# Fold buffers at fixed places inside the up-product buffers, and a new order of steps, in a fused Nyström attention and multiplicative FFN kernel

## The chip, the cores and the metric

The kernel runs on one core of one Trainium2 chip. The metric is device time in microseconds. Five engines take part, each with a queue of its own that it works off in order: TensorE (PE: matmuls, each with a weight load, PEld), VectorE (DVE), ScalarE (ACT), GpSimd (POOL) and SyncE (SP), which here issues transfers only. POOL and ACT issue some as well.

## The reference

```python
# attention: q, k, v are (8, 8, 576, 64); m = 32 landmarks, scale = 1/8
q_lm = q.reshape(B, H, m, S // m, D).mean(axis=3); k_lm = ...   # likewise
A, Bm, C = sm(q, k_lm), sm(q_lm, k_lm), sm(q_lm, k)             # softmax(scale * a @ b.T)
Z = Bm.T / (norm1(Bm) * norminf(Bm) + 1e-6)
for _ in range(6): Z = 2 * Z - Z @ Bm @ Z
x = (A @ Z @ C @ v)           # then heads side by side: (4608, 512)
# multiplicative feed-forward
out = ((x @ w1) * (x @ w2)) @ w3 @ w_out
# w1, w2: (512, 1024); w3: (1024, 1024); w_out: (1024, 512); all float32
```

## The kernel before

**The fold.** Since nothing stands between w3 and w_out, the kernel multiplies them first into w34 (1024 x 512) and needs one product afterwards. Each operand is split into two fp16 parts (high and low), so a block takes three matmuls. `split(c)` (S, L508) makes the two halves of w_out block c in the tile `wsp`. `turned_w3(j, cc)` (T, L515) transposes four 128x128 pieces of w3 block j on PE (L523), and ACT (L527) and DVE (L529) write the two halves to a `w3t` tile. `product(j)` (F, L533) runs 24 matmuls (L537) in eight steps and copies the result to w34 (L540). `load_w3` (L) and `load_wout` (LO) fetch the float32 blocks into `w3f` (three buffers) and `wof` (six buffers).

**The attention**, batch by batch (8 batches, all 8 heads at once): loads of q and k in halves (LQ, LK, on POOL's queue), of v (LV, on SP's), turns on DVE (TQ, TK, L165), landmark sums (SQ, SK: on DVE for batch 0, else on POOL, L194 to L205), `exchange` (E, L212/L223), scores of landmarks (B), norms (N), squares (R), six steps of the inverse (I0 to I5, for one to three batches together), scores C and A (L280, L333), values (V, L347), normalise (M, L366 to L375), landmark_values (Z, L415 to L423).

**The feed-forward.** `project` (G0 to G3, L438) forms Z C v w1 and Z C v w2 for a batch (32 landmarks of each head); ACT (L443) or DVE (L445) writes it to `gt`. `up(st, j)` (U0 to U7) multiplies ahat with one 128-column part of each projection (L453), ACT copies the first (a_sb, L458) and DVE multiplies it with the second, into `ab` (L460): a tile of 8 x 1152 for two batches, two buffers. `down(n)` (W, 36 of them, 128 rows each) multiplies ab with w34 (L495), ACT writes o_sb (L501), and SP sends it out in two pieces (L505). The last, n = 35, is cut into two halves (L476 to L490).

**Memory.** The fold's tiles (`wsp`, four `w3t`, three `w3f`, six `wof`) lie in a pool `pf`. The `ab` buffers lie in a pool `pab` that is opened when the first U is met, after `pf` has been closed: they take its place, and the first U can write only when the fold's tiles have been read for the last time. PSUM holds three tiles `big` of two banks, one bank `small` (scores_b, norms, squares, landmark_values and product 1) and one bank `acc` (the other products, and the downs).

**The order.** Nothing is scheduled automatically. Each of the functions above is a generator, and the string `ORDER` names, word by word, which one goes on by one step. The instructions enter each engine's queue in that order. K is one warm-up matmul, KC one step of `constants()` (L605), GT a tiny copy on POOL that waits for a weight block and so holds back the loads queued behind it, FV and P the same before v of batch 0 and w3 block 4, LW a half load of w1 or w2. The first loads (w3 blocks 0 and 1, w_out blocks 0 to 5) and the load of ACT's function table stand ahead of ORDER.

```python
    for word in ORDER.split():
        if word not in live:
...
            work = started(word)
...
            live[word] = work
        if live[word] is not None:
            next(live[word], None)
```

Of the kernel before, what the change touches and what calls it, by code (L numbers as in the profile page):

```python
# [7 lines left out]
FP32 = mybir.dt.float32  # L8
# [6 lines left out]
B = 8  # L15
H = 8
# [16 lines left out]
T0.0 S.0 S.0 T0.0 T0.0 T0.0 T0.1 S.2 S.2 LQ0.0 T0.1 K LQ1.0 S.1 T0.1 L.2 LO.6 S.3 F.0 K F.1 S.1  # L33
LK0.0 T0.0 KC F.0 LK1.0 T0.0 T1.0 F.0 T1.0 S.3 S.4 K T1.0 S.5 S.4 F.1 K FV.0 F.1 F.0 T1.1 T1.1 K S.6
F.0 S.5 T1.1 KC LO.7 KC F.1 F.1 T1.2 F.1 TQ1.0 T1.2 GT.0 LK1.1 L.3 T0.2 LK0.1 S.7 F.0 S.6 F.1 TQ0.0
T0.2 F.0 GT.2 S.7 T0.2 F.0 SQ0.0 T1.2 F.1 TK1.0 F.0 LQ1.1 LQ0.1 T1.3 P.4 T1.3 F.2 T1.3 F.2 SQ1.0
T0.3 GT.3 TK0.0 F.2 P.4 T0.3 LK1.2 SK0.0 L.5 F.2 T0.3 F.2 F.2 F.2 LK0.2 F.2 F.2 T0.4 F.1 T1.5 LQ1.2
KC SK1.0 F.3 F.3 T0.4 T1.5 F.3 TK0.1 FV.0 F.3 GT.4 T0.4 LW.1 TK1.1 L.6 E.0 F.3 F.3 E.0 B.0 T1.5 B.0
C.0 GT.5 F.3 B.0 F.3 C.0 N.0 T0.5 KC T1.4 TQ1.1 N.0 LW.0 F.3 T1.4 T1.4 SK0.1 C.0 TQ0.1 F.4 LV2.1 F.4
T0.5 F.4 A.0 T0.5 R.0 R.0 R.0 F.4 F.4 F.4 LQ0.2 A.0 I0.0 I0.0 T0.6 LV0.1 SK1.1 L.7 I0.0 A.0 T0.6 C.0  # L40
F.4 I1.0 M0.0 LQ1.3 I1.0 F.4 I1.0 I2.0 T0.6 KC SQ0.1 LW.0 F.4 T1.6 M0.0 F.5 F.5 I2.0 GT.6 I2.0 SQ1.1
M0.0 M1.0 C.0 TK1.2 F.5 V.0 V.0 TQ1.2 M1.0 T1.6 I3.0 F.5 F.5 TK0.2 I3.0 F.5 M1.0 I3.0 LK0.3 F.5 T0.7
F.5 T1.6 V.0 I4.0 V.0 F.5 T0.7 LV1.3 I4.0 F.6 F.6 E.1 F.6 TQ0.2 I4.0 I5.0 E.1 F.6 F.6 I5.0 T1.7 Z.0
SK0.2 Z.0 F.6 T0.7 A.1 Z.0 A.1 T1.7 F.6 F.6 TQ1.3 LQ0.3 A.1 SK1.2 LV3.1 LW.1 LK0.4 G2.0 G0.0 F.6 F.7
T1.7 F.7 G0.0 M0.0 C.1 TQ0.3 LK1.3 SQ0.2 M1.0 G2.0 F.7 C.1 F.7 F.7 C.1 F.7 F.7 C.1 C.1 LQ0.4 G3.0
SQ1.2 G1.0 E.2 E.2 LV1.1 F.7 U0.0 G3.0 B.1 U0.0 G1.0 V.1 U0.0 U4.0 B.1 V.1 TK0.3 U4.0 B.1 V.1 U0.0
U1.0 U4.0 N.1 TK1.3 V.1 LQ1.4 U5.0 U1.0 U4.0 N.1 U5.0 U5.0 U1.0 U2.0 U5.0 U2.0 SK0.3 U1.0 R.1 U3.0
R.1 R.1 U2.0 U3.0 LQ0.5 I0.1 U3.0 LK0.5 SK1.3 U2.0 I0.1 I0.1 U7.0 U3.0 I1.1 F.7 U7.0 I1.1 TK0.4 I1.1
U6.0 W.0 LV0.2 M1.1 U6.0 U6.0 M1.1 U6.0 U7.0 I2.1 U7.0 M0.1 M1.1 M0.1 W.0 I2.1 I2.1 A.2 LV2.2 LK1.5
LK1.4 W.0 I3.1 I3.1 W.1 A.2 I3.1 I4.1 M1.1 M0.1 I4.1 A.2 W.1 I4.1 W.1 I5.1 TQ0.4 I5.1 C.2 Z.1 C.2  # L50
Z.1 I5.1 M0.1 W.2 C.2 Z.1 G0.1 TQ1.4 TK1.4 G1.1 W.2 G0.1 W.0 G1.1 U0.1 U2.1 LV1.2 C.2 U0.1 U0.1 U1.1
W.2 U1.1 SQ0.3 SQ1.3 C.2 W.3 G2.1 SQ0.4 LV3.2 U0.1 U2.1 G3.1 G2.1 V.2 V.2 V.2 U2.1 G3.1 V.2 U1.1
U2.1 SQ1.4 U1.1 U3.1 LQ1.5 U3.1 W.3 TQ0.5 U3.1 SK0.4 U4.1 E.3 SK1.4 LV1.4 U3.1 Z.2 W.3 M0.2 U4.1 Z.2
U7.1 M0.2 U7.1 M0.2 LV2.4 LK1.6 U4.1 E.3 E.4 TK0.5 U5.1 U4.1 U7.1 LV3.3 W.2 LQ0.6 U6.1 U7.1 LV2.3
U5.1 LV3.4 U6.1 Z.2 W.4 E.4 TQ1.5 M1.2 M1.2 U5.1 U6.1 TK1.5 U5.1 B.3 G2.2 M1.2 U6.1 G1.2 G2.2 G0.2
G1.2 W.4 M0.2 G0.2 A.3 M1.2 W.4 G3.2 A.3 A.3 G3.2 LQ1.6 B.3 SK0.5 W.3 W.1 W.5 U3.2 U3.2 C.3 B.3
LQ1.7 C.3 W.5 N.3 LK0.6 W.4 SK1.5 U2.2 LV0.3 LQ0.7 U0.2 C.3 U0.2 N.3 LK1.7 C.3 R.3 U3.2 W.5 U3.2
U0.2 U2.2 U0.2 W.6 SQ0.5 U2.2 U4.2 U2.2 R.3 SQ1.5 U4.2 C.3 W.6 M0.3 M0.3 U1.2 U1.2 W.6 U4.2 U6.2
TQ0.6 V.3 U4.2 U6.2 R.3 V.3 U1.2 U1.2 U6.2 U6.2 W.7 LK0.7 U5.2 I0.3 W.7 U5.2 I0.3 U7.2 I0.3 TQ1.6
I1.3 TK0.6 I1.3 U7.2 W.7 V.3 U7.2 I1.3 W.5 I2.3 W.8 V.3 I2.3 I2.3 TK1.6 W.7 U7.2 I3.3 I3.3 I3.3 W.8  # L60
M1.3 I4.3 I4.3 W.8 LV0.4 U5.2 I4.3 W.9 U5.2 M1.3 I5.3 W.8 M1.3 A.4 M0.3 A.4 W.9 W.9 I5.3 I5.3 M1.3
Z.3 SK0.6 Z.3 A.4 W.6 W.9 C.4 W.10 M0.3 C.4 Z.3 G3.3 W.10 C.4 W.10 G1.3 G3.3 C.4 G0.3 G2.3 W.11 G0.3
U2.3 G1.3 G2.3 U1.3 U2.3 C.4 U2.3 V.4 U1.3 U2.3 SK1.6 E.5 U1.3 U0.3 TQ0.7 V.4 V.4 SQ0.6 LV2.5 U0.3
LV1.5 U1.3 E.5 TQ1.7 M0.4 V.4 U3.3 M0.4 U3.3 M0.4 U3.3 W.11 U0.3 TK0.7 U3.3 U5.3 TK1.7 W.11 U4.3
# [640 lines left out]
```

## Time and profile before

| what | value |
|---|---|
| runs shown, us | 260.65, 261.73, 262.62 (median 261.73) |
| profiled execution: span, us | 260.5; no separate time is given for it |
| granted TensorE clock, mean | 0.998 |
| instructions in the span | 10306 |
| PE / DVE / ACT / POOL busy, us | 249.7 / 161.5 / 159.2 / 119.3 |
| moved by DMA | 37.37 MB, mean 143 GB/s |
| costliest groups on PE, us busy | up L453 74.3; down L495 66.7; fold L537 41.6 |

The profile is one execution. Its page gives busy time by engine, the span in 40 slices, the chain of work that ended last, and groups of instructions by line (count, busy time, mean of one, and what ended the idle time in front of them). The trace behind it also answers by window, by line and by tile, and has the times at which transfers landed. Ends of matmuls are modelled, so a busy PE may still start matmuls slower than it could: the distance between the starts is the safer number.

### The profile page before, as it was taken

Reading aid. Unit: us, or ns where it says so; the run is one execution under the profiler, and the core shown is the slowest. Engines: PE = TensorE matmul, PEld = TensorE weight load, DVE = VectorE, ACT = ScalarE, POOL = GpSimd, SP = SyncE. Lnnn points to the kernel's source line nnn. Section 1 sums busy time; section 2 is a strip of 40 time slices with the busy share of each in tenths; the row PEclk is TensorE's granted clock in tenths of the full one; section 3 lists DMA queues with packets and bytes.
Section 4 is the critical chain, followed back from the end, with each engine's and each line's share of the span. In section 5 each row is a group of like instructions: output and inputs, shape, how many; then the busy total and the mean of one; then the engine's idle time right before and its main releaser. Section 6 shows DMA issues by size and latency. Waiting matters only on the chain.

```text
span 260.5 us, 10306 instructions
## 1 busy us (share of the span) xinstructions
PE 249.7 (96%) x4480; PEld 147.9 (57%) x4480; DVE 161.5 (62%) x306; ACT 159.2 (61%) x349; POOL 119.3 (46%) x199
## 2 busy tenths in 40 slices
PE   6999999989999999899999999999999999999993
PEld 2555554544476558546654764667666465756642
DVE  1579986526687787677658766466474643464510
ACT  3553363525656875995458899847764856456431
POOL 8060697989359989999079796000000000000000
PEclk9999999999999999999999999999999999999999
DMA  6999999999828827999346293130057231621355
GB/s 235 277 305 289 256 257 245 203 169 211 129 72 124 157 63 136 215 250 244 52 111 137 62 258 97 43 87 3 6 126 159 65 81 43 142 65 40 84 115 127
DMA packets 23357, 37.37 MB, mean 143 GB/s; under 512 B 2832, under 2 KB 11536, under 8 KB 23312
## 3 DMA queue, kind: packets, MB, share of 16 engines
q1 hardware_dynamic: 12928, 24.26, 35.6%
q0 software_dynamic: 9792, 11.54, 27.2%
q10 hardware_dynamic: 592, 0.92, 1.0%
q8 instruction: 35, 0.57, 0.9%
q14 instruction: 10, 0.08, 0.1%
HBM read 38.80 MB, written 9.44 MB: 185 GB/s over the span
## 4 chain that ended last, share of the span: by engine, by line
PE 82%; DVE 7%; ACT 5%; DMA 2%; issue 2%; SPq 0%; DVEq 0%; ACTq 0%
PE big L453 21%; PE acc L495 20%; PE acc L537 13%; PE big L438 5%; PE big L347 4%; PE big L389 4%; PE big L523 3%; PE small L537 2%; ACT a_sb L458 2%; DVE ab L460 2%; PE big L366 2%; PE big L495 1%; DMA wof<-in_moe_w_out_dram 1%; PE small L415 1%; PE big L326 1%
## 5 line engine op out<-in xcount | busy, mean ns | idle before, releaser
L453 PE MATMUL big<-ahat,gt 128*128 128x288 f16 x512 | 74.3, 286 | 1.3 <-ACT a_sb L458 0.7
L460 DVE TENSOR_TENSOR ab<-a_sb,big 128x576 f16<-128x576 f16 x64 | 47.1, 750 | 35.3 <-PE big L453 33.5
L495 PE MATMUL acc<-w,ab 128*128 128x512 f16 x264 | 66.7, 380 | 0.0
L453 PEld LDWEIGHTS <-gt 128*128 128x128 f16 x512 | 48.5, 98 | 22.0 <-issue 3.0
L458 ACT CAST a_sb<-big 128x576 f16<-128x576 f32 x64 | 40.2, 639 | 33.2 <-PE big L453 18.8
L194 POOL TENSOR_TENSOR tr<-qkT 128x256 f32<-128x256 f16 x56 | 37.3, 697 | 18.2 <-DVE qkT L165 16.3
L537 PE MATMUL acc<-wsp,w3t 128*128 128x512 f16 x168 | 41.6, 384 | 0.0
L495 PEld LDWEIGHTS <-ab 128*128 128x128 f16 x280 | 25.4, 98 | 27.0 <-issue 4.8
L537 PEld LDWEIGHTS <-w3t 128*128 128x128 f16 x192 | 18.4, 100 | 19.8 <-issue 3.1
L501 ACT ACTIVATE o_sb<-acc 128x512 f32<-128x512 f32 x33 | 19.8, 599 | 10.8 <-PE acc L495 9.5
L445 DVE TENSOR_SCALAR gt<-big 128x1024 f16<-128x1024 f32 x16 | 19.4, 1220 | 7.9 <-PE big L438 7.9
L165 DVE STREAM_TRANSPOSE qkT<-qkn 128x576 uint32<-128x576 uint32 x32 | 24.0, 762 | 0.0
L200 POOL TENSOR_TENSOR tr<-tr 128x256 f32<-128x256 f32 x28 | 19.8, 727 | 0.1
L443 ACT ACTIVATE gt<-big 128x1024 f16<-128x1024 f32 x16 | 15.7, 1024 | 3.4 <-PE big L438 3.3
L438 PE MATMUL big<-wup,zt 64*32 64x512 f16 x512 | 17.3, 379 | 0.3 <-ACT en L370 0.2
L347 PE MATMUL big<-vt,ent 64*32 64x64 f32 x1152 | 14.8, 225 | 0.1
L128 POOL DMA_DIRECT2D qkn<-in_k_dram x16 | 11.5, 722 | 6.9 <-DVE qkT L165 6.9
L347 PEld LDWEIGHTS big<-vt,ent 64*32 64x32 f32 x1152 | 12.7, 105 | 3.4 <-issue 2.3
L284 DVE STREAM_TRANSPOSE ent<-en 128x576 f32<-128x576 f32 x16 | 12.0, 762 | 3.3 <-ACT en L280 3.3
L375 DVE TENSOR_TENSOR ahat<-eat,en 128x576 f16<-128x576 f16 x16 | 13.8, 870 | 0.0
L280 ACT ACTIVATE en<-big 128x288 f32<-128x288 f32 x32 | 12.8, 415 | 0.5 <-PE big L269 0.5
L527 ACT ACTIVATE w3t<-big 128x512 f16<-128x512 f32 (+1 forms) x17 | 9.6, 571 | 5.6 <-PE big L523 5.3
(184 smaller groups left out, 302.8 us busy)
## 6 DMA issues: line engine op xcount, KB each, us to landing
out_dram<-o_sb SPq DMA_DIRECT2D x70, 128.0 KB, 2.4
qkn<-in_q_dram POOLq DMA_DIRECT2D x16, 288.0 KB, 8.5
qkn<-in_k_dram POOLq DMA_DIRECT2D x16, 288.0 KB, 8.9
vt<-in_v_dram SPq DMA_DIRECT2D x16, 288.0 KB, 4.8
vt<-in_v_dram SPq DMA_DIRECT2D x32, 144.0 KB, 4.6
w3f<-in_moe_w_dram SPq DMA_DIRECT2D x6, 512.0 KB, 9.1
wup<-in_moe_w_dram POOLq DMA_DIRECT2D x4, 512.0 KB, 14.7
wof<-in_moe_w_out_dram SPq DMA_DIRECT2D x6, 256.0 KB, 7.4
```

Of the source, the lines that this page charges most:

```text
L165: nc.vector.transpose(out=st["qkT"][:, t, prs].rearrange("p c r q e -> p (c r q e)").bitcast(U32), in_=st["qkn"][:, t, prs, :].rearrange(" ...
L194: add(out=tr[:, c], in0=x[:, c, 0:4, :], in1=x[:, c, 4:8, :], op=ALU.add)
L200: add(out=tr[:, c, 0:2, :], in0=tr[:, c, 0:2, :], in1=tr[:, c, 2:4, :], op=ALU.add)
L347: nc.tensor.matmul(psV[32 * o:32 * o + 32, qd, 0:64], ent[sl, pr, r, :], vt[sl, pr, 64 * r:64 * r + 64], start=(r == 0), stop=(r == RT - 1 ...
L438: nc.tensor.matmul(psG[o:o + 32, qd, :], zt[rs, i, h, :], wup[rs, h, w, fs], start=(i == 0), stop=(i == 1), tile_position=(64 * qd, o))
L445: nc.vector.tensor_scalar(out=g[:, :, w, fs], in0=psG, scalar1=1.0 / ZS, scalar2=None, op0=ALU.mult)
L453: nc.tensor.matmul(p[:, c, 0:HS], st["g"][:, qd, w, 128 * j:128 * j + 128], st["ahat", qd][:, c, :], start=(qd == 0), stop=(qd == 1))
L458: nc.scalar.copy(out=a_sb, in_=p[:, :, 0:HS])
L460: nc.vector.tensor_tensor(out=st["ab"][:, j, st["t0"]:st["t0"] + S].rearrange("p (c s) -> p c s", c=2), in0=a_sb, in1=p[:, :, 0:HS], op=AL ...
L495: nc.tensor.matmul(pso[:, :], ab[:, j, t0:t0 + 128], w34[:, j, :], start=(j == 0), stop=(j == 7))
L501: nc.scalar.activation(out=o_sb, in_=pso, func=AXF.Copy, scale=1.0 / (X64 * X64))
L537: nc.tensor.matmul(psW, w3ts[j, c // 4][:, a, c % 4, :], wsp[:, b, c, :], start=(c == 0 and a + b == 0), stop=(c == 7 and a == 1))
```

## The change

Four things change.

1. *Places.* The two up-product buffers, `abx` and `aby`, now exist from the start, and the fold's tiles are slices of them: `wsp` and one `w3t` lie in abx; the six `wof`, one `w3f` and one `w3t` (used once) lie in aby. Two `w3t` and two `w3f` have places of their own. Batches 0 and 1 write aby, 2 and 3 abx, 4 and 5 aby, 6 and 7 abx. From block 4 on, w3t rotates over three places; from block 3 on, w3f over two.
2. *PSUM.* `small` and `acc` become one name, `one`, with two buffers.
3. *Small instructions.* `squares` makes sz first and tz from it, for all batches in one instruction each (before: tz by one instruction per half and batch from PSUM). The tile `eye` goes; `bt` holds the unit matrix.
4. *Order.* ORDER is another one throughout. The leading loads and the table load become words of it (H, LO, AT). w_out block 3 is still issued from ACT's queue, now behind the table load, and shares a completion semaphore with the first half of w3 block 1, for whose landing its issue waits. Only the head of ORDER is shown.

```diff
 ORDER = """
-T0.0 S.0 S.0 T0.0 T0.0 T0.0 T0.1 S.2 S.2 LQ0.0 T0.1 K LQ1.0 S.1 T0.1 L.2 LO.6 S.3 F.0 K F.1 S.1
-LK0.0 T0.0 KC F.0 LK1.0 T0.0 T1.0 F.0 T1.0 S.3 S.4 K T1.0 S.5 S.4 F.1 K FV.0 F.1 F.0 T1.1 T1.1 K S.6
...
+H.0 LO.0 H.3 LK0.0 KC AT K LO.3 LO.1 K T0.0 T0.1 H.1 K P.4 LO.2 KC H.2 S.0 S.0 S.1 T0.0 T0.0 T0.1 K
+H.4 S.2 K T0.1 S.1 LO.5 F.0 T0.0 F.1 S.2 T0.0 S.3 F.1 T1.0 LO.4 T0.0 F.0 F.1 S.3 LK1.0 LQ1.0 S.4 L.2
...
-    def small():
-        return psp.tile([128, 512], FP32, name="small", bufs=1)
-
-    def acc():
-        return psp.tile([128, 512], FP32, name="acc", bufs=1)
+    def one():
+        return psp.tile([128, 512], FP32, name="one", bufs=2)
...
-        tz_ = ch["tz"] = pz.tile([128, 6, 32], FP32, name="tz_", bufs=2)
-        for i in range(2 * n):
-            nc.vector.scalar_tensor_tensor(out=tz_[:, i], in0=psR[:, 64 * i:64 * i + 32],
-                                           scalar=ch["nrn"][:, i:i + 1], in1=eye2, op0=ALU.mult, op1=ALU.add)
-        yield
         sz_ = ch["sz"] = pz.tile([128, 6, 64], FP32, name="sz_", bufs=2)
         nc.vector.tensor_tensor(out=sz_[:, x], in0=psR[:, 0:128 * n].rearrange("p (x m) -> p x m", m=64),
                                 in1=ch["nrn"][:, x].unsqueeze(2).to_broadcast([128, 2 * n, 64]), op=ALU.mult)
+        yield
+        tz_ = ch["tz"] = pz.tile([128, 6, 32], FP32, name="tz_", bufs=2)
+        nc.vector.tensor_tensor(out=tz_[:, x], in0=sz_[:, x, 0:32],
+                                in1=eye2.unsqueeze(1).to_broadcast([128, 2 * n, 32]), op=ALU.add)
...
-        w3t = w3ts[j, cc] = pf.tile([128, 2, 4, 128], FP16, name="w3t", bufs=4)
+        i = 2 * j + cc
+        w3t = w3ts[j, cc] = (w3t_at[i] if i < 4 else w3t_at[(i - 4) % 3]).rearrange(
+            "p (i c j) -> p i c j", i=2, c=4)
...
-    def open_ab(b):
-        if b // 2 not in pairs:
-            pairs[b // 2] = pab[0].tile([128, 8, 2 * S], FP16, name="ab")
-        sts[b]["ab"] = pairs[b // 2]
-        sts[b]["t0"] = S * (b % 2)
+    def open_ab(st):
+        b = st["b"]
+        st["ab"] = (aby, abx)[b // 2 % 2].rearrange("p (j t) -> p j t", j=8)
+        st["t0"] = S * (b % 2)
...
-    pf_scope = tc.tile_pool(name="pf", bufs=2)
-    pf = pf_scope.__enter__()
+    pf = ctx.enter_context(tc.tile_pool(name="pf", bufs=1))
+    abx = pf.tile([128, 16 * S], FP16, name="abx")
+    aby = pf.tile([128, 16 * S], FP16, name="aby")
...
-    wsp = pf.tile([128, 2, 8, DM], FP16, name="wsp", bufs=1)
+    wsp = abx[:, 0:16 * DM].rearrange("p (i c n) -> p i c n", i=2, c=8)
+    w3t_at = [pf.tile([128, 1024], FP16, name=f"w3t{i}") for i in range(2)] + [
+        abx[:, 16 * DM:16 * DM + 1024], aby[:, 16 * DM:16 * DM + 1024]]
+    w3f_at = [pf.tile([128, DF], FP32, name=f"w3f{i}") for i in range(2)] + [
+        aby[:, 12 * DM:16 * DM].bitcast(FP32)]
+
+    def place_w3(j):
+        w3f[j] = w3f_at[(0, 1, 2, 0, 1, 0, 1, 0)[j]]
...
-        wof[c] = pf.tile([128, DM], FP32, name="wof", bufs=6)
+        c6 = 2 * DM * (c % 6)
+        wof[c] = aby[:, c6:c6 + 2 * DM].bitcast(FP32)
...
+    def table():
+        nc.scalar.add_instruction(mybir.InstLoadActFuncSet(
+            name=nc.get_next_instruction_name(), act_func_set_id=6, engine=mybir.EngineType.Activation))
+        nc.scalar.activation(out=ready, in_=ident[:, 0:1], func=AXF.Copy, scale=WS)
+
+    def lead(n):
+        eng = nc.scalar if n == 3 else nc.sync
+        load_w3(n // 3, (slice(0, 256), slice(256, 512), slice(512, 1024), slice(0, 512), slice(512, 1024))[n], eng)
...
-            for qd in range(2):
-                nc.vector.tensor_copy(out=eye[sl, qd, :], in_=ident[sl, sl])
-            yield
-        nc.vector.tensor_tensor(out=eye2, in0=eye[:, 0], in1=eye[:, 0], op=ALU.add)
-        for i in range(6):
-            nc.vector.tensor_copy(out=bt[:, i, 32:64], in_=eye[:, 0])
+            nc.vector.tensor_copy(out=bt[sl, 0, 32:64], in_=ident[sl, sl])
+            yield
+        nc.vector.tensor_tensor(out=eye2, in0=bt[:, 0, 32:64], in1=bt[:, 0, 32:64], op=ALU.add)
+        for i in range(1, 6):
+            nc.vector.tensor_copy(out=bt[:, i, 32:64], in_=bt[:, 0, 32:64])
...
-            if word[0] == "U":
-                if not pab:
-                    pf_scope.__exit__(None, None, None)
-                    pab.append(ctx.enter_context(tc.tile_pool(name="pab", bufs=2)))
-                open_ab(int(word[3:]))
```

More of the change, by code (lines that the diff above doesn't have):

```diff
@@ L38 @@
[L38 to L52, printed above, removed]
@@ L85 @@
+W.33 W.32 W.27 W.32 W.34 W.27 W.33 W.34 W.35 W.32 W.34 W.31 W.33 W.32 W.31 W.35 W.31 W.34 W.35 W.35
+W.31 W.35 W.35
 """
@@ L230, in scores_b @@
     def scores_b(ch):
-        psB = small()
+        psB = one()
         n = ch["n"]
@@ L287, in norms @@
     def norms(ch):
-        psN = small()
+        psN = one()
         n, x = ch["n"], slice(0, 2 * ch["n"])
@@ L300, in squares @@
     def squares(ch):
-        psR = small()
+        psR = one()
         n, x = ch["n"], slice(0, 2 * ch["n"])
@@ L352, in values @@
         for qd, o, pr, sl in tiles:
-            nc.tensor.matmul(psV[32 * o:32 * o + 32, qd, 64:65], eye[sl, 0, :],
+            nc.tensor.matmul(psV[32 * o:32 * o + 32, qd, 64:65], bt[sl, 0, 32:64],
                              st["sums"][sl, pr:pr + 1], start=True, stop=True,
@@ L412, in landmark_values @@
     def landmark_values(st):
-        psZ = small()
+        psZ = one()
         for qd in range(2):
@@ L459, in up @@
                 yield
+        open_ab(st)
         nc.vector.tensor_tensor(
@@ L473, in down @@
                 c = slice(256 * half, 256 * half + 256)
-                pso = acc() if half else big()[:, 0, :]
+                pso = one() if half else big()[:, 0, :]
                 for j in range(8):
@@ L492, in down @@
             return
-        pso = big()[:, 0, :] if n > 30 and n % 2 else acc()
+        pso = big()[:, 0, :] if n > 30 and n % 2 else one()
         for j in range(8):
@@ L533, in product @@
     def product(j):
-        psW = small() if j == 1 else acc()
+        psW = one()
         for c in range(8):
@@ L598 @@
     mask4 = consts.tile([128, 4, 32], FP32, name="mask4")
-    eye = consts.tile([128, 2, 32], FP32, name="eye")
     ones4 = consts.tile([128, 128], FP16, name="ones4")
@@ L625, in paced_w3 @@
     def paced_w3(j):
-        w3f[j] = pf.tile([128, DF], FP32, name="w3f", bufs=3)
+        place_w3(j)
         nc.gpsimd.tensor_copy(out=w3f[j][:, 0:1], in_=sts[0]["qkn"][:, 1, 0, 0:1])
@@ L645, in started @@
             "S": lambda: split(n), "T": lambda: turned_w3(n, i), "F": lambda: product(n),
-            "P": lambda: paced_w3(n), "L": lambda: load_w3(n), "LO": lambda: load_wout(n, nc.sync),
+            "P": lambda: paced_w3(n), "L": lambda: load_w3(n), "LO": lambda: load_wout(n, nc.scalar if n in (0, 3) else nc.sync),
+            "H": lambda: lead(n), "AT": lambda: table(),
             "FV": lambda: first_v(), "LV": lambda: load_v(st, n, (i,)),
```

103 lines of the change are left out of this document (51 added, 52 removed).

## The prediction

> **What bounds the kernel now.** I read the page's busy shares first, then busy time by stretch, then the chain of work that ended last in order of time, then who waited for whom on PE, then single stretches of the timeline.
>
> ```profile
> PE 249.7 (96%) x4480; PEld 147.9 (57%) x4480; DVE 161.5 (62%) x306; ACT 159.2 (61%) x349; POOL 119.3 (46%) x199
> ...
> PE   6999999989999999899999999999999999999993
> ```
>
> TensorE has work nearly always, and the other engines a third of their time free. A shorter ACT or DVE instruction therefore pays only where PE stands still. Busy time by stretch shows where that is:
>
> ```profile
> 0.00:10.60 10.60, 8.26 (x23) 3.64 (x24) 3.73 (x13) 4.92 (x9) 5.31 (x19) 1.00 0.82 247
> 10.60:30.00 19.40, 19.40 (x107) 10.89 (x106) 16.43 (x37) 8.13 (x15) 6.67 (x14) 1.00 1.13 291
> 30.00:60.00 30.00, 27.88 (x472) 15.43 (x471) 18.74 (x47) 12.84 (x34) 26.71 (x45) 1.00 1.10 219
> ...
> 180.00:250.00 70.00, 69.90 (x1157) 42.46 (x1156) 37.51 (x57) 42.87 (x83) 0.00 (x0) 1.00 0.35 78
> 250.00:260.50 10.50, 6.42 (x38) 3.48 (x36) 0.42 (x1) 2.28 (x5) 0.00 (x0) 0.96 0.58 132
> ```
>
> The second number of a row is PE busy: 2.3 us are missing in the first stretch, 2.1 in the third, 4.1 at the end. The DMA share (last but one) is over 1 until 60 us: the transfers are the tight resource of the fold. The start, on PE:
>
> ```profile
> 4.16 0.66 PE L523 MATMUL big<-ident,w3f 128*128 128x128 f32 x2
> 5.97 1.54 PE L523 MATMUL big<-ident,w3f 128*128 128x128 f32 x6 [1.15 <-DVE w3t L529]
> ...
> 7.73 1.49 PE L537 MATMUL acc<-wsp,w3t 128*128 128x512 f16 x3
> ...
> 10.63 0.60 PE L537 MATMUL acc<-wsp,w3t 128*128 128x512 f16 x2
> ```
>
> Until 10.6 us a 128x512 matmul starts 0.43 us after the one before, from there 0.216. And the chain that ended last, at 35 to 40 us and at 52:
>
> ```profile
> 35.25 0.31 DVE eye L615
> 35.56 2.21 DVE bt L617 x6
> 37.78 0.68 DVE qkT L165
> ...
> 39.02 0.60 DVE w3t L529
> 39.66 0.52 PE big L326 x30
> ...
> 52.42 0.95 issue
> ```
>
> Six copies of constants stand in front of the w3t eviction on DVE, and the scores of batch 0 (A.0, L326) wait for it: PE stands for 1.24 us. At 52.0 it stands for 1.1 us with no releaser in the profile.
>
> I priced every pair of neighbouring matmuls at the median start-to-start time of that pair of lines (trace after 10.7 us). From the first matmul at 1.19 us this gives 241.7 us; the trace has 255.2. The 13.4 us between are PE's waits, by 20 us of PE work: 5.2, 1.4, 1.3, 0.8, 1.3, 0.7, 0.1, 1.3, 0.8, 0.4 and then none. That is all that a better order can win.
>
> **The change, part by part.**
>
> *PE work.* No matmul is added or dropped, 12 warm-ups stay. The new order priced alike is 0.2 us shorter: **-0.2**.
>
> *The head.* q and k pieces are issued after a pause: P.4's copy on POOL now stands behind the first k piece and waits for it (first landing before: 10.9). Weights come sooner: two pieces of 288 KB less lie ahead of the last w_out block, 2.1 us at the 276 KB/us of the first 11 us, so it lands near 16.5 and not 18.6. Against that, wof[3] is now issued from ACT's queue behind the table load and must wait for the first half of w3f[1], whose completion semaphore it shares (5.24 in the trace); S.0 stands behind it on ACT and starts near 5.7 instead of 4.23. First product: S.0 and S.1 (0.63 each), T0.0 (0.39), DVE's 0.42 after it, 7.8 us against 7.73. PE is then 3.7 to 4.7 us behind its priced work, before 5.2. But this is not kept. S.7's second half leaves DVE at 18.0 (16.5 + 0.63 + 0.69 and hops; before 20.6). Behind it DVE now has, with before's durations: eye2 0.31, five copies to bt 1.85, a turn 0.69, two memsets 0.46, L194 1.15, a w3t eviction 0.65, the k sums 1.94, two turns 1.43, an eviction 0.65, L194 1.15, the q sums 1.95: 12.2 us, so the landmarks of batch 0 are ready at 30.2 and exchange E.0 runs then. E.0 is at 25.4 of the priced work, so PE is 4.9 behind; before 31.7 against 26.5, 5.2. **-0.3** (from -1.5, if DVE is ready sooner, to +1).
>
> *Constants out of the path at 35 us.* Six copies become five and stand 15 us earlier (their price is in the 12.2). Between E.0 and A.0 only small waits are left: A.0's second bank waits for ACT's four exponentials, 1.5 us of L280 behind B.0's; I take 0.15 of 1.24: **-1.1** (0 to -1.24). Next late is the eviction of A.0 (0.65 twice), after which I.0 starts with some 0.3 to spare. The 16 small instructions of tz (0.24 each, L311) become 4, and tz now follows sz: DVE is the shorter by 3 us, and idle 38% of the time, so nothing is booked.
>
> *The wait at 52.0.* Unknown cause, so between 0 and -1.1; half: **-0.55**.
>
> *w3f and w3t buffers.* From w3 block 5 on only two places are left of three, and three of w3t. L.6 can be issued only when T1.4 is through, at 32.2 of the priced work, and T0.6 reads it at 38.9: 6.7 us for 512 KB. Before, it was issued at 24.5 and read at 45.5. SP's queue (L.6 and L.7), and the page's row of whole blocks with their median to landing:
>
> ```profile
> 24.49 0.35 SPq L566 DMA_DIRECT2D w3f<-in_moe_w_dram  x1
> ...
> 36.18 0.35 SPq L566 DMA_DIRECT2D w3f<-in_moe_w_dram  x1
> ```
>
> ```profile
> w3f<-in_moe_w_dram SPq DMA_DIRECT2D x6, 512.0 KB, 9.1
> ```
>
> These took 6.2 to 13.8 us by the landings. The 13.8 had 1.15 MB of v ahead in the same queue; once the transfer ahead had landed the last two took 2.6 and 4.0. In the new order L.5 and v's first pieces (22.5 on; 4.2 + 7.2 us by before's landings, and 1.8 for two pieces of batch 2) are through at about 37, when L.6 is issued: 5 to 6 us with the hop, no stall. With before's 9.5 the stall is 2.8. I take **+0.6**, ends 0 and 7.1.
>
> *v of batch 1.* Batch 2's first pieces take the spare v tile, so batch 1's six can start only after V.0: 50.7 to V.1 at 61.8 of the priced work, 11 us. Issue 3.9 us, the last landing 4.5 to 8.9 later (rows at 55.4 and 57.1): 0 to 1.7 late, **+0.4**.
>
> *Up under the fold and shared PSUM banks.* U0 starts at 60.3 of the work instead of 62.8, with 15 products still to run, so PE has filler; a product's or a down's bank may be reused out of turn. I listed for every wait of PE on ACT or DVE how far the PE work in between falls short of the instructions queued there (row durations plus 0.42 us for both hops). After 60 us of work the shortages sum to 7.4 before, where the trace has 5.4 of waits, and to 5.4 now: 4.0, so -1.4. At U0's start, however, ACT has gt (1.02), Ln (0.65), a_sb (0.64), four small exponentials (1.3) and gt again in one line, and U1 and U5 wait in turn; that adds 0.5. **-0.9** (-2.5 to +1.5).
>
> *The tail.* Down 31 now ends between the halves of down 35, and its two issues (0.59 each) stand on SP before the last one: **+0.5** (0 to 0.6). The 4.1 us after PE's last matmul stay.
>
> Sum: -0.2 - 0.3 - 1.1 - 0.55 + 0.6 + 0.4 - 0.9 + 0.5 = -1.55. The profiled execution has a span of 260.5 and no separate time; the runs shown have a median of 261.73, 1.2 above it, within their spread of 2. Against the median this is **260.2 us**.
>
> **Rivals.**
>
> *The w3 load is late.* L.6 takes the 13.8 us that it took before: stall 7.1, where 0.6 was booked, so 266.7. For: all six whole blocks took longer than the 6 us that I need. Against: the backlog ahead of it is gone by my count. It decides against the change from 8.8 us on (stall 2.1), and is over 1% slower from 11.4. The Trainium skill's page DMA: Bandwidth & Descriptors (Queues, rings and completion order) says that each DMA engine takes one queue's descriptors in ring order and goes round between the queues; by that rule L.6 can't pass v's pieces and shares with POOL's queue, which gives this rival's time if the backlog lasts. The landings agree: L.6 came 2.6 us after the last v piece.
>
> *More is won.* E.0 isn't held by DVE (-1.2 more), the 52.0 wait goes wholly (-0.55), no load is late (-1.0): 257.4. For: DVE has 12 fewer instructions. Against: E.0 stood right behind DVE's last sum before too (31.32 and 31.67).
>
> *The waits come back elsewhere.* The order is new in every place; if its later waits sum to before's 5.4 and A.0 waits as before, the -0.9 and -1.1 go: 262.2. For: the large waits at 107.3 (0.82) and 161.2 (0.57) stand at places that no short distance explains.
>
> **How the numbers follow.** Forecast 0.38 (its own range 258.8 to 261.5), more won 0.27, waits back 0.20, late load 0.15. About 1% is what a measurement of this kernel can tell from no change: 259.1 and 264.3. Faster: 0.27 and a quarter of the forecast, 0.36. Slower: most of the late load and a quarter of the waits, 0.20. Same: 0.44. Range 256.5 to 264.5: a little under the second rival, and into the lower end of the late load.
>
> **What would show it.** Right: E.0 (the two L212 matmuls) near 30, DVE's sums of batch 0 ending just before; no DVE copies before A.0; T0.6 (L523, near 44) without a wait; U0's first matmul near 66 to 67, before 70.7. Wrong: PE idle for microseconds before an L523 or before V.1's first L347; PE's last matmul after 257.

## The result, and the profile after

The changed kernel takes 260.07 us (median of 15 runs, 258.44 to 261.60), the kernel before 261.75 (15 runs, 260.65 to 262.62). The ratio is 0.9928, with a 95% interval of 0.9902 to 0.9954: 1.7 us, 0.7%, faster. The forecast was 260.2.

The profiled execution is the quickest of the 15: 258.44 us with a span of 256.7. In all of them the time is about 1.75 us above the span; so the trace of before, span 260.5, is of an execution of some 262.3 (an estimate), 0.5 above its median. The spans differ by 3.8 us, the medians by 1.7: the two traces overstate the gain, and part of the question is what the other 14 runs lose again.

Busy time by stretch of the changed kernel (the second number of a row is PE busy, the last but one the DMA share):

```profile
0.00:10.60 10.60, 7.95 (x35) 3.82 (x36) 4.37 (x15) 4.29 (x8) 3.20 (x16) 1.00 0.80 260
10.60:30.00 19.40, 18.33 (x96) 9.48 (x93) 16.70 (x40) 7.60 (x14) 8.54 (x16) 1.00 1.13 279
30.00:60.00 30.00, 29.14 (x510) 16.86 (x510) 18.98 (x39) 14.36 (x38) 27.94 (x45) 1.00 1.03 197
...
180.00:250.00 70.00, 69.92 (x1037) 42.18 (x1036) 34.43 (x51) 39.86 (x75) 0.00 (x0) 1.00 0.33 76
250.00:256.70 6.70, 2.23 (x15) 1.17 (x13) 0.42 (x1) 0.70 (x2) 0.00 (x0) 0.98 0.55 122
```

From 30 to 60 us PE misses 0.9 us and not 2.1. From 10.6 to 30 it now misses 1.1, where it missed nothing: the fold starts sooner and then waits for DVE, 0.5 us at 13 and 0.8 at 15 us.

With every pair of matmuls priced as in the prediction, PE's waits sum to 9.2 us (before 13.3, the sum of the prediction's list). By 20 us of priced work: 4.7, 1.4, 0.3, 0.9, 0.35, -0.15, 0.2, 0.7, 0.6, 0.1 and then about none. The first 40 us of work have 0.5 us less of waits than before, the next 20 have 1.0 less, the rest 2.6 (2.8 against 5.4).

The places that the prediction named, on PE, in order: E.0 (L210), A.0 (L323), T0.6 (the L523 at 44.99), V.1 (L344 at 69.01):

```profile
30.17 0.39 PE L210 MATMUL big<-lm,pick 128*128 128x256 f16 x2
...
34.86 0.57 PE L323 MATMUL big<-qkT,lm 32*32 32x288 f16 x20
...
44.99 0.63 PE L523 MATMUL big<-ident,w3f 128*128 128x128 f32 x4 [0.86 <-ACT sz__694 L399]
```

```profile
67.32 1.02 PE L450 MATMUL big<-ahat,gt 128*128 128x288 f16 x7
68.27 0.32 PE L344 MATMUL big<-vt,ent 64*32 64x64 f32 x10
69.01 0.59 PE L344 MATMUL big<-vt,ent 64*32 64x64 f32 x36 [0.41 <-DMA vt<-in_v_dram]
```

E.0 is at 30.17. The scores of batch 0 follow without a wait. T0.6 stands for 0.93 us over its priced step, V.1 for 0.62. The first up ran at 66.70 (in the kernel before at 70.74). So the prediction's sign "T0.6 without a wait" failed; those for E.0, the constants and the first up held. The end, PE's last matmul to the last instruction, took 4.4 us (in the kernel before 4.1).

### The profile page after: what moved, and what is told of

Its sections match the earlier page's. It is cut to its first block, busy times and chain, and to the rows that moved or that the text cites. A ratio compares the mean times of both kernels' runs of the same rounds, so it can differ in the third digit from the quotient of the medians.

```text
span 256.7 us, 10307 instructions
## 1 busy us (share of the span) xinstructions
PE 247.1 (96%) x4480; PEld 147.7 (58%) x4480; DVE 158.9 (62%) x289; ACT 158.9 (62%) x349; POOL 116.1 (45%) x199
## 4 chain that ended last, share of the span: by engine, by line
PE 84%; DMA 9%; ACT 2%; DVE 2%; issue 1%; SPq 1%; ACTq 0%; DVEq 0%
PE big L450 25%; PE one L493 23%; PE one L537 11%; PE big L435 6%; PE big L344 5%; PE big L386 4%; DMA vt<-in_v_dram 3%; DMA aby<-in_moe_w_out_dram 2%; PE big L523 2%; DMA w3f<-in_moe_w_dram 2%; PE big L323 1%; PE big L363 1%; PE big L267 1%; PE one L412 1%; DMA out_dram<-o_sb 1%
## 5 line engine op out<-in xcount | busy, mean ns | idle before, releaser
L458 DVE TENSOR_TENSOR abx<-a_sb,big 128x576 f16<-128x576 f16 x32 | 23.6, 752 | 21.8 <-PE big L450 16.4
L493 PE MATMUL one<-w,aby 128*128 128x512 f16 x144 | 37.0, 380 | 0.0
L458 DVE TENSOR_TENSOR aby<-a_sb,big 128x576 f16<-128x576 f16 x32 | 23.7, 750 | 16.9 <-PE big L450 14.2
L537 PE MATMUL one<-abx,w3t 128*128 128x512 f16 x120 | 29.9, 380 | 0.5 <-ACT w3t L527 0.5
L493 PE MATMUL one<-w,abx 128*128 128x512 f16 x120 | 30.0, 379 | 0.0
L499 ACT ACTIVATE o_sb<-one 128x512 f32<-128x512 f32 x33 | 19.6, 602 | 7.0 <-PE one L493 5.6
L442 DVE TENSOR_SCALAR gt<-big 128x1024 f16<-128x1024 f32 x16 | 19.4, 1216 | 7.1 <-PE big L435 7.1
L493 PEld LDWEIGHTS <-aby 128*128 128x128 f16 x144 | 12.8, 98 | 13.0 <-issue 2.7
L493 PEld LDWEIGHTS <-abx 128*128 128x128 f16 x136 | 12.9, 98 | 12.7 <-issue 1.5
L537 PEld LDWEIGHTS <-w3t 128*128 128x128 f16 x120 | 11.1, 98 | 12.3 <-ACT w3t L527 1.0
L344 PE MATMUL big<-vt,ent 64*32 64x64 f32 x1152 | 16.2, 224 | 0.5 <-DMA vt<-in_v_dram 0.4
L344 PEld LDWEIGHTS big<-vt,ent 64*32 64x32 f32 x1152 | 13.8, 105 | 3.9 <-issue 2.3
L537 PE MATMUL one<-abx 128*128 128x512 f16 x60 | 15.5, 379 | 0.4 <-DVE abx L510 0.4
```

The lines of the kernel that those rows point to most:

```text
L344: nc.tensor.matmul(psV[32 * o:32 * o + 32, qd, 0:64], ent[sl, pr, r, :], vt[sl, pr, 64 * r:64 * r + 64], start=(r == 0), stop=(r == RT - 1 ...
L442: nc.vector.tensor_scalar(out=g[:, :, w, fs], in0=psG, scalar1=1.0 / ZS, scalar2=None, op0=ALU.mult)
L458: nc.vector.tensor_tensor(out=st["ab"][:, j, st["t0"]:st["t0"] + S].rearrange("p (c s) -> p c s", c=2), in0=a_sb, in1=p[:, :, 0:HS], op=AL ...
L493: nc.tensor.matmul(pso[:, :], ab[:, j, t0:t0 + 128], w34[:, j, :], start=(j == 0), stop=(j == 7))
L499: nc.scalar.activation(out=o_sb, in_=pso, func=AXF.Copy, scale=1.0 / (X64 * X64))
L537: nc.tensor.matmul(psW, w3ts[j, c // 4][:, a, c % 4, :], wsp[:, b, c, :], start=(c == 0 and a + b == 0), stop=(c == 7 and a == 1))
```

## The experiments

| kernel | us, median (runs) | ratio to before, 95% interval | span of its trace |
|---|---|---|---|
| changed kernel | 260.07 (15) | 0.9928 [0.9902, 0.9954] | 256.7 |
| after_again | 259.41 (6) | 0.9899 [0.9867, 0.9931] | 257.7 |
| before_again | 261.89 (1) | - | 260.1 |
| before_consts_early | 261.13 (12) | 0.9981 [0.9959, 1.0003] | 259.3 |
| block6_place2 | 258.95 (6) | 0.9906 [0.9881, 0.9931] | 257.8 |
| v1_first | 259.68 (12) | 0.9938 [0.9914, 0.9962] | 259.5 |
| both | 258.17 (6) | 0.9864 [0.9837, 0.9892] | 254.9 |
| up_after_fold | 260.13 (12) | 0.9943 [0.9923, 0.9963] | 259.0 |
| both_up_after_fold | 260.26 (6) | 0.9935 [0.9916, 0.9955] | 258.5 |
| both_tail | 258.19 (6) | 0.9878 [0.9846, 0.9910] | 256.2 |
| before_order_fixed | 268.02 (6) | 1.0242 [1.0214, 1.0270] | 267.5 |
| before_order_places | 264.21 (8) | 1.0101 [1.0066, 1.0135] | 261.9 |
| before_32_more | 264.62 (1) | - | 262.8 |

**The two kernels once more: which waits are the order's, which are chance?**

after_again: no edit.

> The changed kernel unaltered, for a second trace and more times: its 15 times so far spread from 258.4 to 261.6 us, three times as wide as their effect. Theory: the spread comes from two transfers that TensorE waits for, the w3 load of block 6 (landed 44.85 us, 0.93 us of wait at 44) and the v pieces of batch 1 (0.87 us of waits at 68 to 70). Then a slower run of this kernel shows its whole excess over 256.7 in these two places, and the waits after 75 us stay at about 2 us by the priced positions. Rival: the excess is spread over many places after 75 us, as waits for DVE and ACT or for nothing that the profile shows.

before_again: no edit.

> The kernel before unaltered, for a second trace. Theory: of its waits, those that its order causes come back at the same place with the same size (1.24 us at 38 to 39.7 before the scores of batch 0), while the wait without a releaser at 52.0 (1.1 us) and the ones at 107.3 (0.82), 115.2 (0.52) and 161.2 (0.56) are chance: they come elsewhere, or not at all. Rival: all come back within 0.1 us, and so are properties of the order.

Of before, my theory fell. Every wait came back within 0.05 us: 1.24 and 1.20 before A.0, 1.11 and 1.08 without a releaser at 52, 0.82 at 107, 0.52 at 115, 0.44 at 158, 0.56 at 161. Only the first 20 us differ (5.2 and 4.6). The one at 107.3, for which I had found no reason, has a plain one: ACT does four copies of landmarks (L223) ahead of the evictions of up, whose bank the next up needs. In before (start, duration, what, and in brackets the wait and its releaser):

```profile
105.89 1.66 ACT L223 COPY lm<-lm 32x256 f16<-32x256 f16 x4
...
107.57 1.18 ACT L458 CAST a_sb<-big 128x576 f16<-128x576 f32 x2
...
108.26 0.94 PE L453 MATMUL big<-ahat,gt 128*128 128x288 f16 x6 [0.66 <-ACT a_sb L458]
```

Of the changed kernel, half held. The second trace is 1.0 us longer: 0.4 in the first 20 us and 0.8 at 68 to 71 us, less some 0.2 in small steps behind it; the wait of T0.6 is the same (0.94). So the place was right for V.1. The cause was not: all pieces of v had landed by 67.8, and PE stood from 69.80 to 71.49 with no releaser:

```profile
69.70 0.31 PE L344 MATMUL big<-vt,ent 64*32 64x64 f32 x10
71.49 0.64 PE L344 MATMUL big<-vt,ent 64*32 64x64 f32 x38 [1.48 <-issue]
```

**The constants, in the order of before.**

```diff
-LQ1.2 KC SK1.0 F.3 ... T0.5 KC T1.4 TQ1.1
+LQ1.2 KC KC SK1.0 F.3 ... T0.5 T1.4 TQ1.1
```

> The kernel before, with the step of its constants that copies the unit matrix into six tiles moved from behind the reciprocals of batch 0 (35 us) to right behind the fourth step (28.8 us), nothing else. Theory of the prediction: the 1.24 us wait before the scores of batch 0 goes, less what the copies now hold up on DVE ahead of the exchange: DVE's sums end 2.5 us later, so the exchange at 31.7 comes up to 2.5 us later. As the prediction books it, the copies are free only where DVE has no chain behind it; here they land in the 12 us chain before the exchange, so no gain, 0 to 1.5 us slower than the kernel before. Rival: the copies are the whole cost of the wait and are hidden at the new place: 1.1 us faster.

The trace shows both effects: A.0's 1.24 us are gone, and E.0 waits 0.39. Waits from 20 to 60 us of work fall from 2.7 to 1.9; the times by 0.5 us, with an interval that just reaches 1. So neither side came out: no loss, and less than the rival's 1.1. The copies were mispriced. They take 0.10 us each here and 0.37 at the old place:

```profile
29.15 0.19 DVE L615 TENSOR_TENSOR eye<-eye 128x32 f32<-128x32 f32 x1
29.26 0.60 DVE L617 COPY bt<-eye 128x32 f32<-128x32 f32 x6
```

The prediction's row has 2.21 us for the same six. At the old place POOL ran three tensor_tensor beside them; here POOL issues DMAs and copies one column. That POOL is the cause is inferred from these two rows.

**The late loads of the changed kernel.** block6_place2:

```diff
-        w3f[j] = w3f_at[(0, 1, 2, 0, 1, 0, 1, 0)[j]]
+        w3f[j] = w3f_at[(0, 1, 2, 0, 1, 0, 2, 1)[j]]
```

> The changed kernel with w3 block 6 in the third place (free since block 2 was turned) and block 7 in the place of block 4; the order of all instructions is kept. So the load of block 6 no longer waits for the turning of block 4. Theory: the 0.93 us wait of TensorE at 44 us is that load's landing (44.85 us), so it goes, and the time falls by 0.9 us against the changed kernel of the same chip. Rival: the wait is for ACT's copy of sz (the releaser that the profile names), and stays.

v1_first (words of ORDER):

```diff
-TQ0.1 LW.0 T0.5 LV3.2 I0.0 ... L.7 T1.6 T1.6 LW.1
+TQ0.1 LW.0 T0.5 LV3.1 I0.0 ... L.7 LV1.1 LV0.1 LV2.1 T1.6 T1.6 LW.1
-Z.0 LV1.1 T1.7 LV3.1 T1.7 ... LQ1.3 F.7 LV0.1 TK1.3 ... G1.0 LV2.1 F.7
+Z.0 T1.7 T1.7 ... LQ1.3 F.7 TK1.3 ... G1.0 LV3.2 F.7
```

> The changed kernel with the spare v tile given to batch 1 instead of batch 2: the two early pieces are those of batch 1, its other four follow block 7's load at about 40 us, and the two pieces of batch 2 come after them. Theory: the waits before the second product with v of batch 1 (0.87 us in the first trace, 1.78 in the second) go, the spread of the times narrows to about 1.5 us, and the median falls by 0.9 to 1.7. Rival: the four pieces now run beside the q and k pieces and the weights of the up products at 40 to 50 us, when the transfers are tight, and delay these: the gain is lost to a wait at 45 to 65 us.

both: these two edits.

> The last two edits together. Theory: they act at different places, so their gains add: 1.8 to 2.6 us less than the changed kernel, 257.5 to 258.5. Rival: with block 6 and the v pieces all early, one of them is late again, and less than either alone is left.

The wait of T0.6 was the load's. In block6_place2 its load is issued at 31.32 and not at 37.34 (SP's queue), and T0.6 (the L523 below) follows the step before it at once, at 44.08, though ACT's copy is where it was:

```profile
43.80 0.34 PE L386 MATMUL big<-sz__644,tz__630 32*32 32x64 f32 x16
44.08 0.66 PE L523 MATMUL big<-ident,aby 128*128 128x128 f32 x4
```

The profile had put the wait down to ACT only because ACT's copy (ending at 44.96) came 0.1 us later than the landing (44.85). The trace of block6_place2 is still longer than the changed kernel's: 0.73 us are new before V.0, where DVE is late (last section), and 1.27 and 0.94 without a releaser at 58.3 and 115.8. In v1_first the wait of T0.6 stays (1.31 us). Its wait for v is gone, and two without a releaser appear at 51.4 (1.28) and 58.6 (1.46). So neither edit alone moves the median beyond its interval. Together they do: 258.17, and the interval (up to 0.9892) lies below that of the changed kernel's 15 runs (from 0.9902), though not below that of its second six. both_tail, the same but for its last words, comes to 258.19. These two are the quickest versions found. In the trace of the kernel both, taken from the quickest of its six executions, PE is busy throughout from 30 to 100 us:

```profile
30.00:60.00 30.00, 30.00 (x515) 17.15 (x513) 19.06 (x40) 15.20 (x39) 28.83 (x45) 1.00 1.11 234
60.00:100.00 40.00, 40.00 (x970) 24.19 (x969) 29.39 (x52) 29.67 (x71) 34.62 (x58) 1.00 0.74 136
```

That isn't so in every execution: the trace of both_tail, with the same words up to there, has two waits without a releaser, 0.67 us at 50.8 and 1.19 at 57.9.

**Up under the fold.** In both kernels the last words of product 7 were put ahead of the first up (in the second, LV3.2 stands for LV2.1):

```diff
-G1.0 LV2.1 F.7 U0.0 M1.1 ... U1.0 F.7 TQ1.3 ... I0.1 F.7 I0.1 ... I1.1 F.7 TK0.4 ... I2.1 F.7 I3.1 ... E.3 F.7 SK0.4
+G1.0 LV2.1 F.7 F.7 F.7 F.7 F.7 F.7 U0.0 M1.1 ... U1.0 TQ1.3 ... I0.1 I0.1 ... I1.1 TK0.4 ... I2.1 I3.1 ... E.3 SK0.4
```

up_after_fold:

> The changed kernel with the five last words of the product of block 7 put ahead of the first up, as before; nothing else is moved. Theory of the prediction: up under the fold is worth part of the 0.9 us booked for it and the shared banks, so 0.3 to 0.9 us slower than the changed kernel, with waits for DVE or ACT between 72 and 82 us. Rival: TensorE had other work in these places too, and the time is the same within 0.2 us: then the gain after 60 us is the order's, not that of up under the fold.

both_up_after_fold:

> The two edits together, and the last words of the product of block 7 ahead of the first up. With the two late transfers out of the way, this gives the price of up under the fold alone. Theory: in up_after_fold the waits of TensorE for DVE and ACT between 70 and 85 us came to 1.75 us, where the changed kernel has none, and hid the late v; so here they stand alone, and the time is 1.0 to 1.8 us more than with both edits. Rival: less than 0.3 us, since other stages take up the same slack later.

In the changed kernel the difference is small and not clear of noise: 0.9943 against 0.9928 and 0.9899. Its trace says why: some 1.7 us of waits for DVE, ACT and the bank between 70 and 85 us are new, but V.1 comes later and no longer waits for its v. With the loads out of the way the price stands alone: 0.9935 against 0.9864, 1.9 us, and PE misses 1.6 us of 60 to 100 us, where both misses none:

```profile
60.00:100.00 40.00, 38.40 (x802) 22.14 (x801) 26.54 (x46) 27.88 (x68) 31.48 (x52) 1.00 0.71 135
```

The difference of the medians is a little above the 1.0 to 1.8 expected.

**The order of before on fixed places.** ORDER is that of before, with the leading loads (H, LO, AT) as words ahead of it; in the second kernel also:

```diff
-        w3f[j] = w3f_at[(0, 1, 2, 0, 1, 0, 1, 0)[j]]
+        w3f[j] = w3f_at[(0, 1, 2, 0, 1, 2, 0, 1)[j]]
-        w3t = w3ts[j, cc] = (w3t_at[i] if i < 4 else w3t_at[(i - 4) % 3]).rearrange(
+        w3t = w3ts[j, cc] = (w3t_at[i % 4]).rearrange(
```

before_order_fixed:

> The changed kernel's functions, fixed fold buffers, shared banks and five constant copies with the order of before (the leading loads as words in front of it): it parts the buffers from the order. Theory: the buffers alone allow, but don't bring: up still begins behind the fold, the constants' step still stands in front of the scores of batch 0, and the waits at 52.0, 107.3, 115.2 and 161.2 stay. Block 6 has one place less to go to, so its load waits for the turning of block 4. 261 to 263 us, no better than before. Rival: the shared banks or the fixed places themselves give the gain, 259 to 260.

before_order_places:

> before_order_fixed was to part the buffers from the order, but there the load of block 6 came ahead of the turning of block 4 in the same place, so that one product was of the wrong block and the time is not that of this order. Here the fixed places are used with the rotation of before (three places for w3, four for its turned halves, up behind the fold). So this is the order of before on fixed places, shared banks, five copies and the joined small steps. Theory: the order carries the gain; the waits at 107 (0.82), 115 (0.52), 158 (0.44) and 161 us (0.56) come back, and the time is 261 to 262.5. Rival: the places, banks and joined steps bring it, and the time is 259 to 260.

Neither computes the reference's result. In the first, block 6 is loaded into the place of block 4 ahead of the turning of block 4, so a product is of the wrong block. In the second, the second half of block 5 is turned into the place of block 3's second half ahead of product 3, and a product stands for 2.0 us at 38 us. And in both the head is another one (one wait of 2.9 us at 4.5). So their totals say nothing on the order. What can be read is the part after 60 us of work, where none of this enters: in the second kernel the waits sum to 5.3 us, in the kernel before to 5.4, and 0.82, 0.52, 0.45 and 0.55 stand at the same four matmuls. Shared banks, fixed places and joined steps do not take them away; another order does. Whether the order alone, in buffers of before, would be as quick wasn't tried: it needs up under the fold, which those buffers forbid.

**The wait without a releaser.** In before:

```diff
     for _ in range(7):
         warm_up()
+    for _ in range(16): nc.tensor.matmul(psw[:, 0, 0:32], warm[:, 0:128], warm[:, 0:32], start=True, stop=True)
```

> The kernel before with 16 short matmuls of 32 columns (16 weight loads and 16 matmuls, 32 more instructions on TensorE) behind the seven leading warm-ups. In all traces so far, TensorE's waits that have no releaser end at an instruction whose number in TensorE's trace leaves 192 when divided by 256: 960 (twice in the kernel before, at 52 us, and in v1_first), 1216, 1728, 3776. Theory: these are late fetches of TensorE's own instructions, 256 to a block; the instruction stream is what counts, so the wait near 52 us comes again in front of instruction 960 of the trace, now a matmul of the product of block 6, 16 matmuls earlier, of 0.5 to 1.5 us, and not in front of the turning of block 7. Rival: the turning of block 7 itself waits for something (its transfer, a copy of ACT): the wait stays in front of it, at instruction 992. About 1 us more than before either way.

It came in front of instruction 960, now inside an inverse step (L389), with 2.26 us. A second came at 149.5 us, in front of 5312, which also leaves 192. The turning of block 7 no longer waits. Both waits and the time were larger than expected: 2.26 us against 0.5 to 1.5, and 264.62 in this one run, 2.7 above the median of before, against about 1.

```profile
49.03 0.33 PE L389 MATMUL big<-sz__721,tz__718 32*32 32x64 f32 x12
51.62 0.30 PE L389 MATMUL big<-sz__721,tz__718 32*32 32x64 f32 x4 [2.26 <-issue]
```

Busy time from the start to the wait counts the matmuls (x behind the first busy time): 473 in before, at another matmul of the program 473 here, and 473 and 601 in v1_first, whose order is another again. 601 is 473 + 128, with as many weight loads: 256 instructions.

```profile
0.00:52.10 52.10, 48.59 (x473) 25.96 (x473) 36.60 (x89) 23.96 (x53) 31.50 (x65) 1.00 1.07 258
```

```profile
0.00:49.20 49.20, 45.89 (x473) 25.34 (x474) 35.85 (x87) 23.65 (x52) 29.63 (x61) 1.00 1.08 260
```

```profile
0.00:51.50 51.50, 47.27 (x473) 24.97 (x474) 36.98 (x86) 23.69 (x54) 32.18 (x64) 1.00 1.07 255
0.00:58.70 58.70, 53.39 (x601) 28.46 (x601) 38.78 (x89) 25.36 (x57) 37.91 (x74) 1.00 1.10 245
```

**The tail.**

```diff
-W.33 W.34 W.35 W.32 W.34 W.31 W.33 W.32 W.31 W.35 W.31 W.34 W.35 W.35 W.31 W.35 W.35
+W.33 W.34 W.31 W.32 W.34 W.33 W.31 W.32 W.31 W.34 W.35 W.31 W.35 W.35 W.35 W.35 W.35
```

> The two edits together, and down 31 finished ahead of the first half of down 35 as in the kernel before, so that no store of it stands on SP ahead of the last ones. Theory: from TensorE's last matmul to the end it is 4.7 us in the changed kernel and 4.4 before; this goes back to 4.4, 0.3 to 0.4 us less than with both edits. Rival: the stores of down 31 are hidden by the last matmuls, and no time is won.

From PE's last matmul to the end it is 4.15 us, with both 4.43: the 0.3 us are there. The medians (258.19 against 258.17) don't show them.

## Why the prediction came out as it did

The time was right to 0.1 us, and the sum less so: four of its eight terms were too small in size (the wait at 52.0, the w3 load, v of batch 1 and, by far the most, up and the banks), and one step stands on two errors that happen to cancel.

*PE work, -0.2.* Held as far as it can be seen: from 180 us on, priced and traced steps agree within 0.5 us in every trace.

*The head, -0.3.* E.0 was forecast at 30.2, 4.9 us behind its priced place; it came at 30.17, 4.8 behind, with DVE's last sum just done, so -0.4. But the chain to it was wrong in two links. "S.7's second half leaves DVE at 18.0": it left at 19.4 (row 18.71, 0.68 us), since splits and w3 evictions go by turns on ACT until 16.4 and on DVE behind it; the last w_out block was there at 14.9 (forecast 16.5; the 276 KB/us used for it is the rate from 6.5 to 13 us, that of the first 10.6 us is 247). And "five copies to bt 1.85": they took 0.52. One is 1.4 late, the other 1.3 short.

```profile
18.71 0.68 DVE L510 SCALAR_TENSOR_TENSOR abx<-aby,abx 128x512 f16<-128x512 f32 x1
19.31 0.19 DVE L614 TENSOR_TENSOR eye<-bt 128x32 f32<-128x32 f32 x1
19.41 0.52 DVE L616 COPY bt<-bt 128x32 f32<-128x32 f32 x5
...
29.62 0.50 DVE L203 TENSOR_TENSOR lm<-tr 128x128 f16<-128x128 f32 x2
```

*Constants out of the path at 35 us, -1.1.* The 1.24 us are gone. before_consts_early shows the step alone in the other order: 0.8 us in its trace.

*The wait at 52.0, -0.55.* It went wholly: -1.1 in this trace. "Unknown cause, so between 0 and -1.1; half" is a choice, not a price. In the kernel before it isn't chance: it came in both its traces and in before_consts_early. It isn't the order's alone either: in before_order_places, the same words in other buffers, the step cost 0.26. The last section has the cause as far as it is known.

*w3f and w3t buffers, +0.6.* Measured +0.93, and 0.90 to 1.31 in the four traces where block 6 has this place. It was issued at 37.34 (forecast 37.1) and landed 7.5 us later (forecast 5 to 6). v's last piece landed at 37.95, so hardly any backlog of its own queue was ahead of it; what was left was to share the engines with POOL's loads, at a DMA share of 1.12 until it landed. The Trainium skill's page DMA: Bandwidth & Descriptors (Queues, rings and completion order), weighed there, has both: order within a queue, turns between queues. The landings agree with it: v's last piece, this load (44.85) and the next (46.58) landed in the order of issue, and from 37.95 to 44.85 us POOL's queue took 66% of the engines and SP's 44%.

*v of batch 1, +0.4.* Measured +0.62 in one trace, 0 in the other (landed at 67.8, read at 68.76).

*Up under the fold and shared PSUM banks, -0.9.* Here the size failed. Waits after 60 us of work fell from 5.4 to 2.8 with V.1's 0.62 still in it: -3.2. "After 60 us of work the shortages sum to ... 5.4 now: 4.0, so -1.4" scaled the waits with a sum of shortages, as if they were spread evenly. But 2.3 us of them are four waits of before at 107, 115, 158 and 161 us, each at one place (at 107 behind ACT's four copies, at 161 behind ACT's exponentials), and the trace of the changed kernel has no wait over 0.25 us after 75 us. And "that adds 0.5" for U0, U1 and U5 did not come: PE had other work. How the 3.2 us divide between the order and up under the fold isn't known: put behind the fold, up costs 1.9 us in the kernel both, whose order was not otherwise changed for it.

*The tail, +0.5.* Measured +0.3.

The sum by the trace is -0.2 - 0.4 - 1.2 - 1.1 + 0.9 + 0.6 - 3.2 + 0.3 = -4.3, where the span fell by 3.8; the other 0.5 lies in steps that aren't placed. The medians differ by 1.7. Of the 2.1 between, 0.5 is that the trace of before is above its median, and 1.6 the median run of the changed kernel loses again. The forecast booked 2.7 us too little and had no term for this loss; that it met the median to 0.1 us is luck. The second trace shows where 1.0 us of the loss goes: 0.4 before 20 us, and 0.8 more at V.1, where a wait of 1.69 without a releaser stands for the 0.62 and 0.25 of the first trace, less the 0.2 behind it. The longest execution of this kernel, 262.05 us, wasn't traced.

Of the rivals, *the w3 load is late* had the right place and the wrong length. *More is won* (257.4) is nearer than the forecast to the profiled execution (258.44), but of its three grounds only the wait at 52.0 held: E.0 is held by DVE, and both loads are late. *The waits come back elsewhere* fell for the trace shown, and is right in one sense: some waits are fixed by no order, and come in one run and not in another.

## What to carry to other kernels

Take a second trace of the kernel before, ahead of any forecast: a wait that returns within 0.05 us belongs to the kernel and is a term of the sum at its full size, one that doesn't return needs a range of its own. Price an instruction from a row with the same neighbour on POOL, not only with the same shape. And when two late transfers are found, mend both before judging either: alone, neither edit here moved the median beyond its interval, since other waits stood in its trace.

## What the runs showed of the hardware

**TensorE waits for its own instructions.** All waits over 0.8 us without a releaser after 20 us, in twelve traces (all but those of before_order_fixed and before_order_places), stand in front of an instruction of PE whose number leaves 192 when divided by 256 (weight loads, matmuls and semaphore waits counted: 960, 1216, 1728, 3776, 5312). Queue q8 of kind "instruction" moves one packet of 16 KB per 256 such instructions, 35 in the kernel. It mostly starts soon after PE enters the block before: 1.1 us after in the median, from 1.3 us ahead to 6.1 after. In before, the one for the block at 960 lies in the stretch from 50.30 to 51.70 us, with the engines otherwise full of POOL's loads (packets, MB, share of the engines):

```profile
q0 software_dynamic: 144, 0.26, 106.1%
q8 instruction: 1, 0.02, 5.7%
```

From the packets and PE's starts in the traces (us):

```
trace            block entered  packet starts  ends    next block reached  PE goes on
before                   47.30         50.33   51.62                52.04       53.36
before_again             46.81         49.92   51.21                51.55       52.85
before_32_more           44.97         48.60   49.97                49.15       51.62
changed kernel           43.91         45.05   46.22                51.12   (no wait)
after_again              65.25         69.05   70.01                69.80       71.49
v1_first                 43.79         49.87   51.30                51.42       52.72
v1_first                 51.42         56.90   58.38                58.64       60.11
both                     43.98         47.08   48.43                50.30   (no wait)
```

PE goes on 1.4 to 1.75 us after the packet's end, in every row with a wait. Twelve traces have 408 such blocks. The 15 whose packet ended less than 1 us ahead of need, or behind it, cost 0.3 to 2.5 us each (one of them also waits for DVE); of those with more than 1.3 us to spare none cost over 0.31, but for six whose wait the profile puts down to a load, ACT or DVE (four of them are T0.6's). Two things make it late: a packet that starts 3 to 6 us after the block before is entered, and a block of many short matmuls (V's 96 of 64 columns pass in 1.3 us). The Trainium skill, on its page Runtime: NRT & Kernel Launch (Instruction fetch mechanics), says that an engine fetches 16 KiB blocks of 256 instructions by its own queue while it runs the block before, and that this is mostly hidden. The size and the way agree with these traces; hidden it is only while the transfers leave room. That the load of the engines delays the packet, two comparisons say. Of the 64 packets that start 3 us or more after the block before is entered, 54 have a DMA share over 1 in the 3 us after that entry; at a share under 0.4 the longest delay of 138 is 1.7 us. And the eight traces of the new order have the same instructions on PE up to the block at 960. In the four where v of batch 1 is asked for at 37 to 42 us (v1_first, both, both_tail, both_up_after_fold) its packet starts 3.1 to 6.1 us after the block before is entered, at a share of 1.03 to 1.10 over the next 4 us; in the other four 1.1 to 2.3 us after, at 0.61 to 0.91.

**DVE behind POOL.** The same product of two f16 tiles (L372) took 0.7 to 1.3 us in most traces, 3.3 in block6_place2 and 3.95 in both_up_after_fold, where POOL's row of four tensor_tensor began 0.16 and 0.27 us behind it; the copies of the constants took 0.37 and not 0.10 us beside POOL. In block6_place2 (the second of the two products begins at 45.91 and takes 3.33):

```profile
45.27 3.96 DVE L372 TENSOR_TENSOR ahat<-eat,en 128x576 f16<-128x576 f16 x2
45.41 0.65 POOL L156 DMA_DIRECT2D wup<-in_moe_w_dram  x1
46.07 2.54 POOL L192 TENSOR_TENSOR tr<-qkT 128x256 f32<-128x256 f16 x4
```

In the changed kernel the second product begins at 45.91 too, but POOL's row 0.78 us behind it, at 46.69, and the product takes 1.22:

```profile
45.26 1.87 DVE L372 TENSOR_TENSOR ahat<-eat,en 128x576 f16<-128x576 f16 x2
```

POOL's four take 2.84 us there and 2.54 in block6_place2. The Trainium skill's page SBUF — State Buffer (Who interferes with whom) has it that the two share a pair of ports under an exclusive lock and that the order of issue decides who waits. That one of the two waits, these rows agree with. The order doesn't come out of the recorded starts: in the traces of the kernels both and after_again POOL's row began first, 0.39 and 0.30 us ahead of the product, and the product took 1.23 and 1.22. In the two slow cases the product ended only after all four of POOL's instructions. So a start that moves by 0.6 us goes with 2 to 3 us on DVE, and 4 to 5 us later with 0.7 (block6_place2) to 1.4 us on PE in front of V.0 (both_up_after_fold).
